# Products of attention pairs with their reciprocals, pinned behind first-layer units

## The chip, the cores and the metric

One Trainium2 chip, one core. The metric is device time in microseconds (us). A core has four engines that compute, each with its own instruction queue that runs in order: TensorE (PE, matrix multiplication), VectorE (DVE), ScalarE (ACT) and GpSimd (POOL). SyncE (SP) only issues transfers here, POOL issues them as well. An engine waits for another by a semaphore.

## What is computed

Three stages in a row: a linear attention, a layer that takes the maximum of three products, and a second feed-forward layer.

```python
def _attn_ref(q, k, v, w_phi):              # q, k, v: 4 batches, 8 heads, 576 tokens, 64
    def phi(x):
        proj = np.einsum('bhsd,df->bhsf', x, w_phi)
        proj = proj - np.max(np.abs(proj), axis=-1, keepdims=True)
        return np.concatenate([np.exp(proj), np.exp(-proj)], axis=-1)
    q_p, k_p = (phi(q), phi(k))
    kv = np.einsum('bhsf,bhsd->bhfd', k_p, v)
    z = np.sum(k_p, axis=2)
    num = np.einsum('bhsf,bhfd->bhsd', q_p, kv)
    den = np.einsum('bhsf,bhf->bhs', q_p, z)[..., None] + 1e-06
    return num / den

def _moe_ref(x, w1, w2, w3, w_out):         # x: 2304 x 512; d_ff 768
    h = np.maximum(np.maximum(x @ w1, x @ w2), x @ w3)
    return h @ w_out

def _moe2_ref(x, w_in, w_out, alpha):       # d_ff 2048
    h = x @ w_in
    return (np.maximum(h, 0.0) + alpha * np.minimum(h, 0.0)) @ w_out
```

Where the change works is the line num / den of the attention, whose result is the x of the first layer.

## The kernel before

Heads are taken in pairs: 4 batches of 4 pairs, 16 in all. An fp32 operand is split into a rounded high part and the rest (hi, lo), and a product is made of three matmuls: weights hi with x hi, weights hi with x lo, weights lo with x hi.

The loop at L458 runs over the pairs. Iteration i loads pair i+1, runs `queries` of pair i-1 interleaved with `keys` of pair i, converts some weights of the first layer, and then runs three units of the first layer (`layer1`), from i = 4 on and with a lag of two units, so that 34 units are done in it. A unit is one half (288 tokens) of one batch times one of six blocks of d_ff; 48 units in all, 12 for a batch. It has three groups, one for each of w1, w2 and w3, and a group is 12 matmuls of 128x288 into one tile p: three for each of the batch's four pairs, with the pair last made in the end. ACT copies the first group's p (s, L441), DVE takes the maximum with the second (s, L442) and the third (ho, L444), and POOL stores ho (L446, into h_d). Batches 1 to 3 are units 12 to 23, 24 to 35 and 36 to 47.

`queries` ends with the division. PE leaves numerators and denominators in nd (ACT copies them there, L362); POOL moves the denominators to dc with two small transfers (L393) and the second head's numerators (L394); DVE takes the reciprocal (L396); POOL writes it to memory (r_d, L398) and reads it back as rows spread over the partitions (xr, L405, two transfers for each half of the tokens); DVE multiplies (xr, L407), ACT rounds to x hi (L70) and DVE makes x lo (L76). Pairs of the first batch but the last do that on POOL. There are three xr buffers, three nd buffers.

After the loop the last pair's `queries` runs, and then the tail loop (L627) with units 34 to 47. Unit 36 is the first that needs the last pair's x. Beside each unit of the tail two steps of `convert` prepare the weights of the following layers: SP loads a tile of 512 KB (st, L498, three buffers, the next load issued when a buffer is freed), ACT converts (wt, L83), DVE has four rows for it (L85, L87, L89 and L91, the last two read st) and forms differences (L519), and POOL parks results in memory (q_d, L532). Then comes the first layer's second product (L679).

What sets the order: the kernel is scheduled ahead of time by a list scheduler that keeps a simulated clock and picks for each engine by priority and readiness; `high_priority` moves a block ahead of others. `keep_in_program_order` keeps an instruction on its engine where the program has it.

Of the kernel before, what the change touches and what calls it, by code (L numbers as in the profile page):

```python
# [14 lines left out]
ALU = mybir.AluOpType  # L15
# [5 lines left out]
B, H, S, D = 4, 8, 576, 64  # L21
NPAIR = H // 2
# [7 lines left out]
CH = S // 2  # L30
# [23 lines left out]
def tile_kernel(ctx: ExitStack, tc: tile.TileContext, qT, kT, tails, v, w_phi, w1, w2, w3, w_out, w_in, w_out2, alpha, out):  # L54
# [11 lines left out]
    nc = tc.nc  # L66
# [8 lines left out]
    def sub(eng, dst, src, hi):  # L75
        eng.tensor_tensor(dst, src, hi.bitcast(F32), op=ALU.subtract)  # L76
# [37 lines left out]
    def bank(tag, bufs, nm):  # L114
        return ps.tile([P, 512], F32, tag=tag, bufs=bufs, name=nm)
# [4 lines left out]
    ap_ctx, lp_ctx = ExitStack(), ExitStack()  # L120
# [3 lines left out]
    def at(shape, dtype, name, tag=None, bufs=1):  # L124
        pool = ap if (tag or name) in KEYS_ONLY else lp
        return pool.tile(shape, dtype, name=name, tag=tag or name, bufs=bufs)
# [34 lines left out]
    def i_of(pair):  # L161
        return pair[0] * NPAIR + pair[1]

    def plain_kv(pair):
        return pair[0] < 2
# [102 lines left out]
    def products(dst, ops, **kw):  # L268
        for i, (x, y) in enumerate(ops):
            nc.tensor.matmul(dst, x, y, start=i == 0, stop=i == len(ops) - 1, **kw)  # L270
# [69 lines left out]
    def queries(pair):  # L340

        parts = ("q",) if plain_kv(pair) else ("qh", "ql")
        qf = []
        for n, (o, w) in enumerate(CHUNKS):
            qf.append([])
            for x in parts:
                tag = f"qh{n}" if x != "ql" and pair[1] % 2 * len(x) != 1 else f"ql{n}"
                qf[n].append(at([P, 2, 2, w], F32 if plain_kv(pair) else F32R, tag=tag, bufs=1, name=x))
        nd = [at([P, S], F32, tag="nd", bufs=3, name="nd") for _ in range(2)]

        def num(n):
            o, w = CHUNKS[n]
            kv = kvs_of[pair]
            for h in range(2):
                pn = bank("p1", 3, "pn") if pair[0] == 0 else bank("pn", 1, "pn")
                ops = []
                for s in range(2):
                    q_ = [t[:, h, s] for t in qf[n]]
                    k_ = [t[:, h, s] for t in kv]
                    ops += [(k_[0], x) for x in q_] + [(x, q_[0]) for x in k_[1:]]  # L360
                products(pn[:, :w], ops)
                A.activation(nd[h][:, o : o + w], pn[:, :w], AF.Copy)  # L362

        def tail():
            yield 2, (0,), tail_of[pair]

        for g, tiles, pp in chain(project_queries(pair), tail()):
            o, w = (0, 2 * P, SM)[g], ST if g == 2 else 2 * P
            pt = bank("pn" if pair[0] == 0 and g == 1 else "pt", 1, "pt")
            for i in range(len(tiles)):  # L370
                for h in range(2):
                    c = h * len(tiles) * P + i * P
                    nc.tensor.transpose(pt[:, c : c + P], pp[:, 2 * i + h], ident)  # L373
            n = min(g, 1)
            dst = [t[:, :, :, o - CHUNKS[n][0] : o - CHUNKS[n][0] + w] for t in qf[n]]
            if plain_kv(pair):
                e = dst[0]
            else:
                e = at([P, 2, 2, 256], F32, tag="qe", bufs=2, name="qe")[:, :, :, :w]
            pv = pt[:, : 256 * len(tiles)].rearrange("p (h s) -> p h s", h=2)[:, :, -w:]  # L380
            A.activation(e[:, :, 0], pv, AF.Exp)
            A.activation(e[:, :, 1], pv, AF.Exp, scale=-1.0)
            if not plain_kv(pair):
                (hi_dve if g == 1 else hi_act)(dst[0], e)
                sub(V, dst[1], e, dst[0])
            yield
            if g != 1:
                num(n)
        yield
        dc = at([P, S // D], F32, tag="dc", bufs=2, name="dc")  # L390
        for h in range(2):
            dr = D * (1 - h)
            nc.gpsimd.dma_start(dc[h * D : (h + 1) * D], nd[h][dr : dr + 1].rearrange("a (p n) -> a p n", p=D))  # L393
        nc.gpsimd.dma_start(nd[0][D:], nd[1][D:])  # L394
        V.tensor_scalar(dc, dc, EPS, None, op0=ALU.add)
        V.reciprocal(dc, dc)  # L396
        rows = r_d[pair[0], pair[1]]
        nc.gpsimd.dma_start(rows.rearrange("h (p n) -> (h p) n", p=D), dc)  # L398
        res = []
        for c in range(2):  # L400
            cs = slice(c * CH, (c + 1) * CH)
            xr = raw_tile()
            for h in range(2):
                r = slice(h * D, (h + 1) * D)
                nc.gpsimd.dma_start(xr[r], rows[h : h + 1, cs].to_broadcast([D, CH]))  # L405
            e = G if i_of(pair) < NPAIR - 1 else V
            e.tensor_tensor(xr, nd[0][:, cs], xr, op=ALU.mult)  # L407
            xh, xl = x_tiles(c)
            if e is G:
                G.tensor_copy(xh, xr)  # L410
            else:
                hi_act(xh, xr)
            sub(e, xl, xr, xh)
            res.append((xh, xl))
        xs[pair[0]].append(res)

    def raw_tile():
        return xs_.tile([P, CH], F32, tag="xr", bufs=3, name="xr")
# [8 lines left out]
    def layer1(b, c, f, x, w, spread=False):  # L427
        pw = []
        for j in range(3):
            if spread:  # L430
                p = bank(("pn", "pt", "kv")[j], 1, "p1")
            else:
                p = bank("p1", 3, "p1")
            ops = []
            for k in range(KT):
                ks = slice(k * P, (k + 1) * P)
                ops += three(w[j][:, 0, ks], w[j][:, 1, ks], *x[k][c])
            products(p[:, :CH], ops)
            pw.append(p)
        s1 = xs_.tile([P, CH], F32, tag="s1", bufs=2, name="s1")  # L440
        A.activation(s1, pw[0][:, :CH], AF.Copy)  # L441
        V.tensor_tensor(s1, pw[1][:, :CH], s1, op=ALU.max)  # L442
        ho = xs_.tile([P, CH], F32, tag="ho", bufs=2, name="ho")
        V.tensor_tensor(ho, pw[2][:, :CH], s1, op=ALU.max)  # L444
        o = b * S + c * CH
        nc.gpsimd.dma_start(h_d[f, :, o : o + CH], ho)  # L446

    pairs = [(b, pr) for b in range(B) for pr in range(NPAIR)]
# [9 lines left out]
    for i, pair in enumerate(pairs):  # L458
        if i + 1 < len(pairs):
            load_pair(pairs[i + 1])  # L460
        with tc.high_priority(offset=(0, SOON, NOW, NOW)[pair[0]]):
            if i == PLAIN - 1:
                hi_dve(wph, wraw)
                sub(V, wpl, wraw, wph)
            run(*([at_priority(LATER, queries(last))] if last else []), keys(pair))
            last = pair
        count = CONVERT_IN[i] if i < len(CONVERT_IN) else 0
        for j in range(count):
            for _ in range(min(count, 4) if j == 0 else int(j + 3 < count)):
                fetch(begun[pair])  # L470
            with tc.high_priority(offset=LAST if i < NPAIR - 1 else 0):
                n = sum(len(x) for x in w)
                run(split_w123(n // 3, n % 3))
        u0 = 3 * (i - NPAIR) - LAG
        for u in range(u0, u0 + 3):
            if u >= 0:
                c, f = (u % 2, u // 2) if u < 12 else (u // NF1 % 2, u % NF1)
                layer1(u // 12, c, f, xs[u // 12], w[f])
    ap_ctx.close()
    sp = ctx.enter_context(tc.tile_pool(reuse_waits="tile", name="sp", bufs=1, side="right"))  # L480
    with tc.high_priority(offset=NOW):
        run(queries(last))
    lp_ctx.close()
    ring2 = ctx.enter_context(tc.tile_pool(reuse_waits="tile", name="ring2", bufs=10, side="right"))
    hp_ctx = ExitStack()
    hp = hp_ctx.enter_context(tc.tile_pool(reuse_waits="tile", name="hp", bufs=1, side="right"))

    def granule(pool, nm):

# [137 lines left out]
    for u in range(3 * (len(pairs) - NPAIR) - LAG, 12 * B):  # L627
        c, f = u // NF1 % 2, u % NF1
        layer1(u // 12, c, f, xs[u // 12], w[f], u % 2 == 0)
        with tc.high_priority(offset=LATER):  # L630
            convert(2)
        if u == 12 * B - NF1 - 1:
            for kk in range(NF1 // 2):
                load_h(0, kk)
            for kk in range(NF1 // 2):
                early.append(fetch_h(1, kk))
# [30 lines left out]
    for c in range(2 * B):  # L667
# [7 lines left out]
        for ms in ((0, 1), (2, 3)) if c == 0 else (range(KT),):  # L675
            for k, m in ((k, m) for k in range(NF1) for m in ms):
                cs = slice(m * P, (m + 1) * P)
# [169 lines left out]
    for block in range(nblocks):  # L847
# [4 lines left out]
        for half in range(2):  # L852
# [5 lines left out]
            for i in ORDER:  # L858
                for f in range(4):
                    ts_ = slice(f * T, (f + 1) * T)  # L860
                    r = wq[2 * half + f // 2, i]
                    cs = slice(f % 2 * 256, f % 2 * 256 + 256)
# [83 lines left out]
```

## Time and profile before

| | us |
|---|---|
| median of three runs | 875.53 |
| the runs | 874.87, 875.53, 876.23 |
| the profiled execution | 875.7 |
| its span | 873.9 |

Busy time over the span is 867.7 us for PE (99%), 683.1 for DVE (78%), 490.4 for ACT (56%) and 158.6 for POOL (18%). The costliest line is the matmul L270 with the tile p, 1728 matmuls of the first layer, 250.4 us of PE. The profile's names leave out buffer numbers, so p or xr stands for all tiles of that name. A line of a helper (L270, L70, L76, L83 to L91) stands for all its callers; the tile's name tells them apart.

### The profile page before, as it was taken

How to read it: one execution, taken by the hardware profiler on the slowest of the kernel's cores; microseconds unless marked ns; L12 is line 12 of the kernel's file. 1: busy time of each engine (PE TensorE's matmuls, PEld its weight loads, DVE VectorE, ACT ScalarE, POOL GpSimd, SP SyncE). 2: the span in 40 equal slices, each digit the busy share in tenths (PEclk: the TensorE clock that was granted, in tenths of full speed). 3: DMA queues.
4: the chain of work that ended last, by engine and by line, in shares of the span. 5: the costliest groups of instructions: out<-in, count | busy, mean ns of one | idle time of the engine just before them, and what ended most of it. 6: DMA issues, size and time to landing. Idle time of an engine off the chain costs nothing.

```text
span 873.9 us, 17484 instructions
## 1 busy us (share of the span) xinstructions
PE 867.7 (99%) x6631; PEld 854.8 (98%) x6631; DVE 683.1 (78%) x1290; ACT 490.4 (56%) x1017; POOL 158.6 (18%) x278
## 2 busy tenths in 40 slices
PE   9999999999999999999999999999999999999998
PEld 8898999999999999999999999999999999999998
DVE  4579888976888878888999755746478999987781
ACT  4666757677777762334455354646477763544440
POOL 0355222202222235521100101111111000000000
PEclk9999999999999999999999999999999999999999
DMA  6445544223323137996578853746248746533321
GB/s 235 134 165 161 170 125 154 64 63 95 92 74 103 37 115 258 323 320 199 178 247 270 258 174 133 241 168 203 109 138 275 261 153 189 171 123 122 121 74 49
DMA packets 70437, 143.00 MB, mean 164 GB/s; under 512 B 9152, under 2 KB 36176, under 8 KB 70352
## 3 DMA queue, kind: packets, MB, share of 16 engines
q1 hardware_dynamic: 53664, 92.95, 34.3%
q0 software_dynamic: 14816, 45.26, 15.1%
q10 hardware_dynamic: 1872, 3.67, 1.2%
q8 instruction: 52, 0.85, 0.4%
q14 instruction: 33, 0.27, 0.1%
HBM read 93.07 MB, written 46.34 MB: 160 GB/s over the span
## 4 chain that ended last, share of the span: by engine, by line
PE 94%; DVE 3%; DMA 1%; ACT 0%; issue 0%; POOL 0%; DVEq 0%; POOLq 0%; ACTq 0%
PE p L270 26%; PE acc L865 21%; PE sums L777 12%; PE p L679 9%; PE pc L777 6%; PE pj L270 5%; PE pn L270 5%; PE kvp L311 3%; PE pb L777 3%; PE kvp L298 3%; PE pt L373 2%; DVE mx L217 1%; DMA dc<-nd 1%; PE kvt L330 0%; PE warm L135 0%
## 5 line engine op out<-in xcount | busy, mean ns | idle before, releaser
L270 PE MATMUL p<-x,w123t 128*128 128x288 f32 x1728 | 250.4, 298 | 0.0
L270 PEld LDWEIGHTS p<-x,w123t 128*128 128x128 f32 x1728 | 234.8, 188 | 1.4 <-DVE ho L444 0.3
L777 PE MATMUL sums<-x,wi 128*128 128x288 f32 x768 | 107.6, 295 | 0.0
L865 PE MATMUL acc<-wq,o 128*128 128x256 f32 x864 | 105.5, 283 | 0.0
L865 PEld LDWEIGHTS acc<-wq,o 128*128 128x128 f32 x864 | 104.2, 189 | 0.0
L777 PEld LDWEIGHTS sums<-x,wi 128*128 128x128 f32 x768 | 103.9, 188 | 0.0
L865 PE MATMUL acc<-wq,x 128*128 128x256 f32 x648 | 78.1, 280 | 0.0
L865 PEld LDWEIGHTS acc<-wq,x 128*128 128x128 f32 x648 | 77.0, 188 | 0.0
L679 PE MATMUL p<-x,wo 128*128 128x288 f32 x576 | 76.6, 295 | 0.0
L679 PEld LDWEIGHTS p<-x,wo 128*128 128x128 f32 x576 | 76.5, 188 | 0.0
L796 DVE SCALAR_TENSOR_TENSOR g<-neg,al,g 128x576 f32<-128x576 f32 x64 | 50.3, 812 | 23.6 <-ACT neg L795 23.6
L217 DVE TENSOR_REDUCE mx<-pj 128x4 f32<-128x512 f32 (+1 forms) x80 | 49.8, 629 | 15.6 <-PE pj L270 15.3
L785 ACT ACTIVATE s<-sums 128x576 f32<-128x576 f32 x48 | 31.1, 647 | 42.0 <-PE sums L777 41.9
L797 POOL DMA_DIRECT2D g_d<-g x32 | 22.9, 715 | 166.8 <-DVE g L796 144.7
L446 POOL DMA_DIRECT2D h_d<-ho x48 | 27.1, 564 | 123.5 <-DVE ho L444 103.5
L83 ACT ACTIVATE wt<-st 128x512 f32<-128x512 f32 x38 | 25.2, 674 | 36.0 <-DMA st<-in_w_out 18.9
L250 ACT ACTIVATE ke<-pj,mx 128x128 f32<-128x128 f32 x96 | 36.6, 382 | 13.8 <-DVE mx L217 13.6
L795 ACT ACTIVATE neg<-g 128x576 f32<-128x576 f32 x64 | 40.2, 676 | 6.2 <-DVE g L827 5.9
L298 PEld LDWEIGHTS kvp<-v,ke 128*128 128x128 f32 x320 | 40.3, 191 | 2.4 <-ACT ke L251 0.5
L298 PE MATMUL kvp<-v,ke 128*128 128x128 f32 x320 | 42.3, 277 | 0.1
L441 ACT ACTIVATE s<-p 128x288 f32<-128x288 f32 x48 | 19.7, 413 | 40.3 <-PE p L270 36.4
L70 ACT ACTIVATE o<-wt 128x512 fp32r<-128x512 f32 x45 | 27.4, 627 | 25.0 <-PE acc L865 15.9
(161 smaller groups left out, 1819.6 us busy)
## 6 DMA issues: line engine op xcount, KB each, us to landing
g_d<-g POOLq DMA_DIRECT2D x32, 576.0 KB, 4.0
a<-g_d SPq DMA_DIRECT2D x36, 512.0 KB, 4.6
st<-in_w_out SPq DMA_DIRECT2D x22, 512.0 KB, 5.2
wst<-in_w SPq DMA_DIRECT2D x18, 512.0 KB, 4.2
st<-in_w_in SPq DMA_DIRECT2D x16, 512.0 KB, 4.3
yr<-y_d SPq DMA_DIRECT2D x28, 288.0 KB, 3.6
v<-in_v SPq DMA_DIRECT2D x16, 480.0 KB, 4.7
q_d<-wt POOLq DMA_DIRECT2D x28, 256.0 KB, 5.9
```

Of the source, the lines that this page charges most:

```text
L70: A.activation(dst, src, AF.Copy)
L217: V.tensor_reduce(mx, pv, axis=AX.X, op=ALU.max, apply_absolute_value=True, negate=True)
L250: A.activation(ev[:, a, 0], pv[:, a], AF.Exp, bias=mx[:, a : a + 1])
L270: nc.tensor.matmul(dst, x, y, start=i == 0, stop=i == len(ops) - 1, **kw)
L298: nc.tensor.matmul(kvp[:, j * P : (j + 1) * P], e[:, c], rv[:, t, j // 2 : j // 2 + 2].rearrange("p a d -> p (a d)"), start=first, stop=t ...
L446: nc.gpsimd.dma_start(h_d[f, :, o : o + CH], ho)
L679: nc.tensor.matmul(p2[m // 2][1][:, m % 2], x, y, start=k + n == 0, stop=k == NF1 - 1 and n == 2)
L777: nc.tensor.matmul(dst[:, j], a, b, start=start and n == 0, stop=n == len(ops) - 1, skip_group_check=True)
L785: A.activation(s, src, AF.Copy)
L795: A.activation(neg, gv[:, j], AF.Relu, scale=-1.0)
L796: V.scalar_tensor_tensor(gv[:, j], neg, al[:, f + j : f + j + 1], gv[:, j], op0=ALU.mult, op1=ALU.add)
L865: nc.tensor.matmul(acc[i], x, y, start=half == 0 and f == 0 and n == 0 and place[i][1] == 0, stop=half == 1 and f == 3 and n == 2, skip_gr ...
```

## The change

The product, the rounding and the difference are taken out of `queries` into a function `make_x`, and `queries` leaves its pair in a list `waiting`. For the first batch's pairs and the last pair of the second and third batch `make_x(False)` is called at once, as before. The other nine pairs of the loop wait until three units of `layer1` have been written, and their products are pinned there with `keep_in_program_order`. The last pair waits for unit 34, the first unit of the tail, and the pools ring2 and hp are opened behind it.

```diff
-        res = []
+        raw = []
         for c in range(2):
             xr = raw_tile()
             for h in range(2):
                 ...
+            raw.append(xr)
+        waiting.append((pair, nd[0], raw))
+        if pair[0] == 0 or pair[1] == NPAIR - 1 and pair != pairs[-1]:
+            make_x(False)
+    waiting = []
+    def make_x(pinned=True):
+        pair, num_, raw = waiting.pop(0)
+        res = []
+        for c, xr in enumerate(raw):
             e = G if i_of(pair) < NPAIR - 1 else V
-            e.tensor_tensor(xr, nd[0][:, cs], xr, op=ALU.mult)
+            x = e.tensor_tensor(xr, num_[:, c * CH : (c + 1) * CH], xr, op=ALU.mult)
+            if pinned:
+                tc.keep_in_program_order(x)
...
                 layer1(u // 12, c, f, xs[u // 12], w[f])
+        if waiting:
+            make_x()
     ap_ctx.close()
...
     with tc.high_priority(offset=NOW):
         run(queries(last))
-    lp_ctx.close()
-    ring2 = ctx.enter_context(tc.tile_pool(reuse_waits="tile", name="ring2", bufs=10, side="right"))
-    hp_ctx = ExitStack()
-    hp = hp_ctx.enter_context(tc.tile_pool(reuse_waits="tile", name="hp", bufs=1, side="right"))
...
     for u in range(3 * (len(pairs) - NPAIR) - LAG, 12 * B):
         c, f = u // NF1 % 2, u % NF1
         layer1(u // 12, c, f, xs[u // 12], w[f], u % 2 == 0)
+        if waiting:
+            make_x()
+            lp_ctx.close()
+            ring2 = ctx.enter_context(tc.tile_pool(reuse_waits="tile", name="ring2", bufs=10, side="right"))
+            hp_ctx = ExitStack()
+            hp = hp_ctx.enter_context(tc.tile_pool(reuse_waits="tile", name="hp", bufs=1, side="right"))
         with tc.high_priority(offset=LATER):
             convert(2)
```

In the changed kernel the product is L419, s is L455 and L456, ho L458, its store L460, the staging load L510, the differences L531 and their parking L544. The orders of all engines are the same up to a group of the first batch at about 108 us, and again from the first matmul of the second product (L679 before) on.

PE, at the joint of the third and the fourth batch. p_5081 is the last group of unit 35; p_5126, p_5139 and p_5152 are unit 36, p_5191, p_5204 and p_5217 unit 37. Before:

```order
L270 MATMUL p_5081<-x,w123t 128x288 x12
L270 MATMUL p_5126<-x,w123t 128x288 x12
L270 MATMUL p_5139<-x,w123t 128x288 x12
L270 MATMUL p_5191<-x,w123t 128x288 x6
L270 MATMUL p_5152<-x,w123t 128x288 x12
L270 MATMUL p_5191<-x,w123t 128x288 x6
L270 MATMUL p_5204<-x,w123t 128x288 x12
```

And now:

```order
L270 MATMUL p_5081<-x,w123t 128x288 x12
L270 MATMUL p_5126<-x,w123t 128x288 x9
L270 MATMUL p_5139<-x,w123t 128x288 x9
L270 MATMUL p_5152<-x,w123t 128x288 x9
L270 MATMUL p_5191<-x,w123t 128x288 x9
L270 MATMUL p_5204<-x,w123t 128x288 x9
L270 MATMUL p_5217<-x,w123t 128x288 x9
L270 MATMUL p_5126<-x,w123t 128x288
L270 MATMUL p_5139<-x,w123t 128x288
```

The six groups of units 36 and 37 are cut behind their ninth matmul, and the rest of them, one and then two matmuls each, follows in turn.

DVE, around the last pair's first product (xr_4963; x_4967 is its x). ho_4767 belongs to unit 31, the s1 behind the product to unit 32. Before:

```order
L444 TENSOR_TENSOR ho_4767<-p1_4751,s1_4764 128x288
L91 SCALAR_TENSOR_TENSOR wt_5372<-st_5256,wt_5372 128x512
L519 TENSOR_TENSOR wt_5381<-wt_5372,wt_5323 128x512
L519 TENSOR_TENSOR wt_5307<-wt_5372,wt_5307 128x512
L85 TENSOR_SCALAR wt_5386<-wt_5386 128x512
L407 TENSOR_TENSOR xr_4963<-nd_4868,xr_4963 128x288
L442 TENSOR_TENSOR s1_4809<-p1_4783,s1_4809 128x288
L87 TENSOR_SCALAR wt_5386<-wt_5386 128x512
L76 TENSOR_TENSOR x_4967<-xr_4963,x_4967 128x288
```

And now. The rows ahead of these, from the back: the two L89, two L87 and two L85 of wt_5443 and wt_5451, and ho of unit 35. Staging tiles take three buffers in turn, in the order st_5321, st_5378, st_5392, st_5449.

```order
L91 SCALAR_TENSOR_TENSOR wt_5443<-st_5321,wt_5443 128x512
L91 SCALAR_TENSOR_TENSOR wt_5451<-st_5378,wt_5451 128x512
L531 TENSOR_TENSOR wt_5459<-wt_5443,wt_5451 128x512
L85 TENSOR_SCALAR wt_5508<-wt_5508 128x512
L87 TENSOR_SCALAR wt_5508<-wt_5508 128x512
L89 SCALAR_TENSOR_TENSOR wt_5508<-st_5392,wt_5508 128x512
L91 SCALAR_TENSOR_TENSOR wt_5508<-st_5392,wt_5508 128x512
L531 TENSOR_TENSOR wt_5517<-wt_5508,wt_5459 128x512
L531 TENSOR_TENSOR wt_5443<-wt_5508,wt_5443 128x512
L85 TENSOR_SCALAR wt_5522<-wt_5522 128x512
L87 TENSOR_SCALAR wt_5522<-wt_5522 128x512
L419 TENSOR_TENSOR xr_4963<-nd_4868,xr_4963 128x288
```

The product has moved from between units 31 and 32 to behind unit 35 and the conversions up to half of wt_5522's.

POOL, from the write of the last pair's reciprocals (r_d) on. ho_4449 is a store of unit 29; ho_5017 is one of unit 34, ho_5097 one of unit 35. Before:

```order
L398 DMA r_d_67<-dc_4956 128x9
L532 DMA q_d_70<-wt_5245 128x512
L532 DMA q_d_70<-wt_5171 128x512
L446 DMA h_d_66<-ho_4449 128x288
L532 DMA q_d_70<-wt_5250 128x512
L532 DMA q_d_70<-wt_5259 128x512
L405 DMA xr_4963<-r_d_67 64x288 x2
L405 DMA xr_4970<-r_d_67 64x288 x2
```

And now:

```order
L398 DMA r_d_67<-dc_4956 128x9
L460 DMA h_d_66<-ho_5017 128x288
L544 DMA q_d_70<-wt_5386 128x512
L544 DMA q_d_70<-wt_5395 128x512
L460 DMA h_d_66<-ho_5097 128x288
L405 DMA xr_4963<-r_d_67 64x288 x2
L405 DMA xr_4966<-r_d_67 64x288 x2
```

The reads of the rows have moved behind the store of unit 35.

## Rows read from the trace of the kernel before

**Rows 1.** The page, 40 slices: granted TensorE clock, tenths of full speed.
```profile
PEclk9999999999999999999999999999999999999999
```

**Rows 2.** Busy us (x instructions) of each engine by stage, clock, DMA share, GB/s.
```profile
60.00:100.00 40.00, 38.44 (x266) 34.82 (x265) 36.15 (x83) 30.04 (x87) 16.40 (x27) 1.00 0.51 157
100.00:338.00 238.00, 238.00 (x1847) 235.67 (x1846) 196.69 (x403) 162.25 (x402) 62.87 (x114) 1.00 0.34 100
338.00:378.00 40.00, 40.00 (x303) 40.00 (x303) 35.71 (x76) 11.15 (x22) 18.23 (x35) 1.00 0.93 316
378.00:436.00 58.00, 57.97 (x438) 57.73 (x438) 53.17 (x112) 25.48 (x50) 10.67 (x19) 1.00 0.68 218
```

**Rows 3.** Chain of work 360 to 440: start us, us, what.
```profile
382.38 53.48 PE p L270 x402
```

**Rows 4.** Timeline, ACT, 374 to 384: start us, us, instruction, [idle before <- releaser].
```profile
375.24 0.41 ACT L441 ACTIVATE s<-p 128x288 f32<-128x288 f32 x1 [2.10 <-PE p L270]
```

**Rows 5.** Timeline, DVE, 364 to 370.
```profile
366.08 0.42 DVE L85 TENSOR_SCALAR wt<-wt 128x512 f32<-128x512 f32 x1
366.41 0.45 DVE L407 TENSOR_TENSOR xr<-nd,xr 128x288 f32<-128x288 f32 x1
```

**Rows 6.** Timeline, ACT, 360 to 368.
```profile
364.85 0.68 ACT L83 ACTIVATE wt<-st 128x512 f32<-128x512 f32 x1 [0.47 <-DMA st<-in_w_out]
366.90 0.45 ACT L70 ACTIVATE x<-xr 128x288 fp32r<-128x288 f32 x1 [1.37 <-DVE xr L407]
```

**Rows 7.** Waits of DVE, whole span: us in total, times, longest us.
```profile
DVE xr L407 <- DMA xr<-r_d: 7.8, 7, 1.8
```

**Rows 8.** Line L405, 300 to 375: issue of the reciprocals' rows to landing.
```profile
DMA to landing us min/median/max: 2.6/3.7/5.1
```

**Rows 9.** Timeline, DVE, 335 to 346.5.
```profile
335.89 0.42 DVE L85 TENSOR_SCALAR wt<-wt 128x512 f32<-128x512 f32 x1
336.34 0.43 DVE L87 TENSOR_SCALAR wt<-wt 128x512 uint32<-128x512 uint32 x1
...
341.49 0.76 DVE L85 TENSOR_SCALAR wt<-wt 128x512 f32<-128x512 f32 x2
342.16 0.45 DVE L444 TENSOR_TENSOR ho<-p,s 128x288 f32<-128x288 f32 x1
342.53 0.75 DVE L87 TENSOR_SCALAR wt<-wt 128x512 uint32<-128x512 uint32 x2
343.19 1.29 DVE L89 SCALAR_TENSOR_TENSOR wt<-st,wt 128x512 uint32<-128x512 uint32 x2
344.40 1.29 DVE L91 SCALAR_TENSOR_TENSOR wt<-st,wt 128x512 uint32<-128x512 uint32 x2
```

**Rows 10.** Line L498, 335 to 385: issue of a staging load to landing.
```profile
DMA to landing us min/median/max: 4.8/6.1/8.8
```

**Rows 11.** Line L498, 300 to 436: the same.
```profile
DMA to landing us min/median/max: 3.3/4.8/8.8
```

**Rows 12.** Timeline, POOL, 340 to 400.
```profile
357.15 2.07 POOL L405 DMA_DIRECT2D xr<-r_d  x4 [0.71 <-DMA r_d<-dc]
359.62 0.57 POOL L446 DMA_DIRECT2D h_d<-ho  x1 [0.40 <-DVE ho L444]
```

**Rows 13.** Timeline, PE, 0 to 14.
```profile
1.05 2.82 PE L135 MATMUL warm<-idle 128*128 128x64 f32 x12 [1.05 <-DVE signs L137]
3.79 3.63 PE L270 MATMUL pj<-wraw,k 128*128 128x256 f32 x8
...
11.37 1.03 PE L270 MATMUL pj<-wraw,k 128*128 128x256 f32 x4
```

**Rows 14.** Busy us by stage, the start: columns as in rows 2.
```profile
4.00:7.40 3.40, 3.40 (x8) 2.31 (x8) 1.93 (x5) 0.00 (x0) 0.19 (x1) 1.00 0.92 264
```

**Rows 15.** Timeline, PE, 60 to 96.
```profile
66.72 1.19 PE L270 MATMUL p<-x,w123t 128*128 128x288 f32 x6
...
84.38 0.39 PE L270 MATMUL pj<-wph,xhk 128*128 128x256 f32 x1 [0.83 <-DVE ppt L221]
```

More of the change, by code (lines that the diff above doesn't have):

```diff
@@ L398, in queries @@
         nc.gpsimd.dma_start(rows.rearrange("h (p n) -> (h p) n", p=D), dc)
-        res = []
+        raw = []
         for c in range(2):
-            cs = slice(c * CH, (c + 1) * CH)
             xr = raw_tile()
@@ L404, in queries @@
                 r = slice(h * D, (h + 1) * D)
-                nc.gpsimd.dma_start(xr[r], rows[h : h + 1, cs].to_broadcast([D, CH]))
+                src = rows[h : h + 1, c * CH : (c + 1) * CH]
+                nc.gpsimd.dma_start(xr[r], src.to_broadcast([D, CH]))
+            raw.append(xr)
[7 more added lines that the diff above has]
+        for c, xr in enumerate(raw):
             e = G if i_of(pair) < NPAIR - 1 else V
-            e.tensor_tensor(xr, nd[0][:, cs], xr, op=ALU.mult)
+            x = e.tensor_tensor(xr, num_[:, c * CH : (c + 1) * CH], xr, op=ALU.mult)
+            if pinned:
+                tc.keep_in_program_order(x)
             xh, xl = x_tiles(c)
```

## Prediction, with its working

> **What bounds the kernel now.** I read the rows in this order: the granted clock, the busy time by stage, the chain around the place where the order changes, then the engines that hand TensorE its data there. The clock is full in all 40 slices [rows 1]. By stages [rows 2], PE is busy 238.00 of 238 us from 100 to 338, all 40 from 338 to 378 and 57.97 of 58 from 378 to 436. A busy engine may still be slow, so I hold the pitch against it: around the joint of loop and tail the chain is matmuls alone, 402 in 53.48 us [rows 3], 0.133 us each. So in the stretch that the change touches (its orders on PE differ only between about 108 us and the first w_out matmul at about 436 us) TensorE is the bound at full speed with nothing to give back. What DVE, ACT or a queue saves there cannot shorten the span; what one of them makes PE wait for lengthens it, one for one, because all later stages follow on PE.
>
> The reader should see the other side as well: how early x is ready. The s copy of unit 35 starts at 375.24, released by that unit's first group [rows 4]; two groups of 12 remain, 24 x 0.133 = 3.2 us, so unit 36, the first that uses the last pair's x, starts at about 378.4. In the kernel before, that pair's first product starts at 366.41 [rows 5] and ACT rounds it to x hi at 366.90, done at 367.35 [rows 6]: 11 us early.
>
> **The change part by part.**
> No work is added or removed: the same products, the same DMAs, the same roundings. Of the nine pairs pinned in the loop, the product now stands on DVE behind the third unit of its iteration. What that removes is DVE standing in front of a product while the reciprocals' rows are on their way: 7.8 us in 7 waits over the whole kernel, none over 1.8 [rows 7]. PE waits for none of them [rows 2], so they are worth 0. What it adds is that these x are ready later. I went through the new orders between 108 and 360 us: wherever a group is split for a missing x, or an nd buffer is freed later by a later product, PE has at least 2 us of other matmuls in front of the need. I take 0. From below the bound is also 0 (PE is full there); from above I take one landing of the rows, 5.1 at the longest [rows 8].
>
> The last pair is another matter. Its product is pinned behind unit 34, and the new order of DVE puts it behind ho of unit 35 and the conversions of that unit and the next. PE's order says what this costs: after unit 35's last group, units 36 and 37 are issued as six pieces of 9, which is what needs three of the four pairs, and only then the matmuls with the last pair's x. That is 54 x 0.133 = 7.2 us of work that doesn't need it. The next matmul needs x hi.
>
> How late is x hi? Clock zero is the end of unit 35's last group.
> - The handover to DVE is 0.04, as from the product (end 366.86) to ACT (366.90) [rows 5, 6]. ho has the product's shape, 0.45 [rows 5]. Together 0.5.
> - Then seven conversion rows up to the L91 that frees the staging buffer: two L85 (from 341.49 to 342.16 with the next row, 0.67), two L87 (342.53 to 343.19, 0.66), two L89 (343.19 to 344.40, 1.21), one L91 (half of the pair's 1.29, 0.65) [rows 9]. 3.2, so 3.7.
> - SP can issue the load of the next staging tile only now: there are three buffers, and st_5449 is the third tile after st_5321, so takes its place. The new order needs this very tile before the product: L85 and L87 of wt_5522 stand ahead of it on DVE, and they need ACT's L83 of that tile. Landing took 4.8, 6.1 and 8.8 us (least, median, most) in 335 to 385 [rows 10], and 3.3, 4.8 and 8.8 in 300 to 436 [rows 11]. I take 6.1, since the load falls into the first of these stretches, where the DMA engines were busy 0.93 of the time [rows 2]. 9.8.
> - L83 takes 0.68 [rows 6]: 10.5. L85 to L87 of one tile is 0.45 (335.89 to 336.34) [rows 9], L87 to the next row 0.33, as 366.08 to 366.41 between an L85 and a product [rows 5]: 11.3. The product, 0.45: 11.7. Handover, x hi in 0.45 [rows 6], handover: 12.3.
>
> So PE stands still for 12.3 - 7.2 = 5.1 us. With the other landings it is 2.3 (3.3 us), 3.8 (4.8) and 7.8 (8.8). While it waits, the conversion rows between (five more, some 3 us) run inside the landing and cost nothing; if the landing were short they would be the cover that is gone, but 3.3 still hides them. What is late next: x lo, one DVE row behind x hi, has six matmuls (0.8 us) in front of it; nothing.
>
> The Trainium skill has a rule for a transfer's time (DMA: Bandwidth & Descriptors, "Anatomy of one DMA — SWDGE (gpsimd) path"): some 2.0 us fixed plus the bytes at 436 GB/s. It is for the GpSimd queue and one DMA by itself; for this 512 KB tile it gives an estimate of 3.2 us, a stall of 2.2, and 877.7. The rows differ from it, 6.1 at the median with the DMA engines nearly full, and I go by the rows.
>
> The other ingredient of the product is the rows of reciprocals. On POOL their issue moves from 357.15 [rows 12] to behind the store of unit 35's ho, so at 0.5 + 0.57 for that store [rows 12], and two issues (half of 2.07) later the first half's DMAs are out: 2.1. Landing takes 2.6 to 5.1, median 3.7 [rows 8]: 5.8. The product, x hi and two handovers add 0.98: 6.8, under 7.2. So POOL's path alone does not stall PE, and with 5.1 it does by 1.0; it is hidden behind the staging load either way. The later stages have room: the conversions for the first w_out matmul are the same in number, and the order from there on is that of before.
>
> Sum: 0 + 0 + 5.1. The profiled run took 875.7 with a span of 873.9 (1.8 around it), so it would come to 880.8 with a span of 879.0; the median of the three runs is 0.2 lower, so I forecast 875.53 + 5.1 = 880.6.
>
> **The rivals.**
> *A, PE falls back to the pace of its start.* After an idle time of 1.05 us PE starts slowly: from 3.79 on eight pj matmuls of 256 columns take 3.63 us (0.454 each), and at 11.37 four take 1.03 (0.258) [rows 13]. The granted clock reads 1.00 in that stretch too [rows 14], full speed or 2.4 GHz, so here the pace tells it and not that column; 0.454 to 0.258 is near the step to 1.2 GHz. In the middle of the kernel I found no idle time longer than 0.83 [rows 15], so no row shows what 5 us does. If PE is slow after the gap for as long as at the start (1.05 to about 7.4, 6.4 us), half of that is lost, 3.2 us: 883.8. For it speaks that the gap would be by far the longest; against it, that no row behind the start shows a fall.
> The Trainium skill (TensorE: Matmul & The Clock Gate, "What's actually happening") says that the throttled state is the default, that activity releases it and idleness brings it back. By that rule A would hold, at 883.8; the start of this trace agrees with its first half only.
>
> *B, no stall.* The staging tile may be there in time after all, if DVE frees its buffer sooner than I think or DVE runs ahead of PE. Then POOL's path decides, 6.8 against 7.2, and the time is 875.5. For it: the least landing, 3.3, leaves 2.3 us, so the whole rest of the chain would have to be 2.3 shorter. Against it: each link stands in the in-order queue of one engine. That the pins do nothing at all (product issued where it was) gives the same 875.5.
>
> *C, more waits.* The nine pins in the loop cost PE too, where I found 2 us of cover; one rows' landing above that cover, 5.1 - 2 = 3.1, in one place gives 883.7.
>
> *D, faster.* Mechanism: DVE freed of its waits before products serves PE sooner between 60 and 100 us, the only stage near the change where PE idles: 38.44 of 40 [rows 2], the longest wait, 0.83, for DVE's ppt [rows 15], and the six matmuls at 66.72 take 1.19 instead of 0.80. All idle time gone is 1.6, with as much again hidden in slow pitches 3.1: 873.9 to 872.4. It decides only if the last pair's x costs under 1.6. Against it: the order of every engine is the same up to about 108 us, and batch 0's products aren't pinned.
>
> **How the numbers follow.** The stall of 2.3 to 7.8 us with the pace held has 0.53 (877.8 to 883.3, 880.6 the middle of it by the median landing); A 0.21 (with the same landings 881.0 to 886.5); C 0.09; B 0.13; D 0.04. The range 877.0 to 886.0 takes in the forecast, C and all but the end of A, and leaves out B, D and that end, under 0.2. A measurement of this kernel tells about 0.2%, 1.75 us, from no change. Faster: D, 0.04. Same: B, 0.13. Slower: the rest, 0.83.
>
> **What would show it.** Right: one idle stretch on PE of about 5 us, 7.2 us behind unit 35's last group (about 385 us into the span), released by ACT's x hi; ahead of it on DVE the product without a wait for xr, behind L85 and L87 that waited for ACT's L83, which waited for an st load; DVE's 7.8 us in front of products mostly gone; before 378 us PE full. A shows as 288-column matmuls at some 0.26 instead of 0.133 just behind, or a granted clock below 1. C shows as PE idle between 110 and 378. Wrong would be: the gap's releaser is POOL's rows or nothing, or the staging tile landed long before DVE came to it.

## Result: 10 us slower, and the profile after

The changed kernel takes 885.43 us (median of four runs, 884.20 to 885.85) against 875.47 for the kernel before; the ratio is 1.0111, with a 95% interval of 1.0093 to 1.0129. Its profiled execution took 885.04, with a span of 883.3; before it was 873.9 [rows 2 to 4 are of that span], so 9.4 us are to be found.

The page of the changed kernel, PE's busy tenths and the granted clock in 40 slices of 22.1 us:

```profile
PE   9999999999999999979999999999999999999998
...
PEclk9999999999999999989999999999999999999999
```

One slice stands out in both, that from 375 to 397: PE at 7 tenths, the clock at 8. By stages (columns as in rows 2):

```profile
100.00:338.00 238.00, 236.64 (x1833) 233.82 (x1832) 189.24 (x385) 156.57 (x389) 55.69 (x102) 1.00 0.31 93
...
385.00:392.00 7.00, 2.22 (x17) 1.99 (x15) 4.84 (x10) 0.97 (x2) 2.85 (x5) 0.89 0.97 331
392.00:400.00 8.00, 7.13 (x38) 7.13 (x39) 7.91 (x19) 4.09 (x9) 1.89 (x3) 0.67 0.96 325
400.00:446.00 46.00, 46.00 (x350) 46.00 (x349) 43.10 (x91) 20.30 (x40) 6.19 (x10) 1.00 0.60 199
```

From 385 to 392 PE works 2.22 of 7 us. From 392 to 400 it is busy again, but the granted clock is 0.67 and 38 matmuls fit where 60 would. From 400 on all is as before. A smaller loss stands far ahead: 236.64 busy of 238 between 100 and 338, where before it was 238.00 [rows 2]. PE's waits (us in total, times, longest) name all three:

```profile
PE p L270 <- ACT x L70: 5.7, 1, 5.7
...
PE p L270 <- ACT w123t L70: 1.0, 1, 1.0
...
PE pn L270 <- ACT nd L362: 0.3, 1, 0.3
```

PE's timeline around the large one (start, us, instruction, idle time before it and who ended it):

```profile
369.73 17.49 PE L270 MATMUL p<-x,w123t 128*128 128x288 f32 x131
392.87 19.38 PE L270 MATMUL p<-x,w123t 128*128 128x288 f32 x129 [5.65 <-ACT x L70]
```

The count closes. Idle time before x hi: 5.65. The chain of waits counts 339 matmuls of L270 in 47.14 us behind the gap; at the 0.133 of [rows 3] they take 45.1, so the slow pace costs 2.05. The two short waits are 1.03 (at 174.42) and 0.34 (at 120.00). Together 9.07 of 9.4; 0.2 more stand in 60 to 100, 38.22 busy in place of 38.44 [rows 2].

Now the chain into x hi. DVE first, from ho of unit 35 on; the order of these rows is that printed ahead of the prediction:

```profile
380.54 0.45 DVE L458 TENSOR_TENSOR ho<-p,s 128x288 f32<-128x288 f32 x1
...
383.48 1.28 DVE L91 SCALAR_TENSOR_TENSOR wt<-st,wt 128x512 uint32<-128x512 uint32 x2
...
387.81 1.29 DVE L531 TENSOR_TENSOR wt<-wt 128x512 f32<-128x512 f32 x2
391.09 0.43 DVE L85 TENSOR_SCALAR wt<-wt 128x512 f32<-128x512 f32 x1 [1.98 <-ACT wt L83]
391.55 0.43 DVE L87 TENSOR_SCALAR wt<-wt 128x512 uint32<-128x512 uint32 x1
391.89 0.45 DVE L419 TENSOR_TENSOR xr<-nd,xr 128x288 f32<-128x288 f32 x1
```

ACT and SP at the same time (ACT: the conversion of that tile, then the rounding to x hi):

```profile
390.39 0.66 ACT L83 ACTIVATE wt<-st 128x512 f32<-128x512 f32 x1 [5.08 <-DMA st<-in_w_out]
392.38 0.78 ACT L70 ACTIVATE x<-xr 128x288 fp32r<-128x288 f32 x2 [1.32 <-DVE xr L419]
```

```profile
384.23 3.94 SPq L510 DMA_DIRECT2D st<-in_w_out  x3
```

Read it from the end. x hi at 392.38 follows the product at 391.89. The product follows L87 by 0.34 and that follows L85 by 0.46, DVE's own pitch. L85 waited 1.98 for ACT's L83 at 390.39, and that waited 5.08 for a staging tile. SP had issued this load at 384.23, right behind the first of the two L91 rows (half of 1.28 from 383.48: 384.12): 6.1 us to landing, the median taken in the prediction [rows 10].

The chain of waits tells it otherwise, and here it misleads. Its last pieces before x hi:

```profile
385.06 6.79 DMA q_d<-wt
391.84 0.05 issue
391.89 0.46 DVE xr L419
```

It puts the product down to a parking transfer (q_d) that landed in the same tenth of a microsecond. The product starts 0.34 behind the row ahead of it, as such rows do when nothing is waited for, and has no idle time in DVE's timeline; the only wait is two rows earlier. The reciprocals' rows, what the product does need from POOL, were issued from 382.53 on and landed 3.5 to 5.6 us later. The first half's two issues are the second row below; they landed 4.4 and 4.0 us after their starts, by 387.1, well ahead of the product:

```profile
377.24 0.54 POOL L398 DMA_DIRECT2D r_d<-dc  x1 [1.13 <-DVE wt L87]
...
382.53 1.05 POOL L405 DMA_DIRECT2D xr<-r_d  x2 [0.40 <-DMA r_d<-dc]
```

```profile
DMA to landing us min/median/max: 3.5/4.2/5.6
```

The first of these two rows is worth more than the second. It is the write of the last pair's reciprocals, and before it stood here:

```profile
350.00 0.54 POOL L398 DMA_DIRECT2D r_d<-dc  x1
```

Now it is at 377.24, 27 us later. Something far ahead of the tail made the pair late.

### The profile page after: what moved, and what is told of

The parts are those of the page before. It is cut to its first block, busy times and chain, and to the rows that moved or that the text cites. A ratio compares the mean times of both kernels' runs of the same rounds, so it can differ in the third digit from the quotient of the medians.

```text
span 883.3 us, 17499 instructions
## 1 busy us (share of the span) xinstructions
PE 869.9 (98%) x6631; PEld 857.0 (97%) x6631; DVE 683.4 (77%) x1290; ACT 488.2 (55%) x1017; POOL 159.8 (18%) x278
## 4 chain that ended last, share of the span: by engine, by line
PE 90%; DMA 4%; DVE 3%; issue 1%; POOL 1%; ACT 1%; SPq 0%; POOLq 0%; ACTq 0%; DVEq 0%
PE p L270 23%; PE acc L883 20%; PE sums L795 12%; PE p L697 9%; PE pc L795 6%; PE pj L270 5%; PE pn L270 5%; PE kvp L311 3%; PE pb L795 3%; PE kvp L298 2%; PE pt L373 2%; DMA dc<-nd 1%; DMA q_d<-wt 1%; DMA r_d<-dc 1%; DMA v<-in_v 1%
## 5 line engine op out<-in xcount | busy, mean ns | idle before, releaser
L270 PE MATMUL p<-x,w123t 128*128 128x288 f32 x1728 | 253.2, 300 | 6.7 <-ACT x L70 5.7
L270 PEld LDWEIGHTS p<-x,w123t 128*128 128x128 f32 x1728 | 236.9, 190 | 8.3 <-ACT x L70 5.9
L460 POOL DMA_DIRECT2D h_d<-ho x48 | 27.8, 580 | 120.3 <-DVE ho L458 107.6
L83 ACT ACTIVATE wt<-st 128x512 f32<-128x512 f32 x38 | 24.9, 671 | 30.6 <-DMA st<-in_w_out 17.0
L362 ACT ACTIVATE nd<-pn 128x256 f32<-128x256 f32 (+1 forms) x64 | 26.8, 424 | 27.1 <-PE pn L270 23.4
L405 POOL DMA_DIRECT2D xr<-r_d x64 | 33.9, 535 | 39.9 <-DMA r_d<-dc 24.7
```

Source lines behind the costliest of these rows:

```text
L405: nc.gpsimd.dma_start(xr[r], src.to_broadcast([D, CH]))
```

## What the experiments tell apart

Two theories. **P** is the prediction's: the pin of the last pair behind unit 34 puts its product behind the conversions. **N** came from those 27 us: the pins in the loop do it. A product that stands behind a unit's ho on DVE holds its numerator's buffer (nd, three of them) until then; the copies of the next pairs' numerators wait for a buffer, and the whole attention chain of the last batch slides back. Times are medians of 4 to 10 runs, ratios are to runs of the kernel before on the same chip.

**The last pair's pin taken out.**

```diff
-        if pair[0] == 0 or pair[1] == NPAIR - 1 and pair != pairs[-1]:
+        if pair[0] == 0 or pair[1] == NPAIR - 1:
             make_x(False)
```

The pools ring2 and hp are opened right behind the last pair's queries again, as in the kernel before.

> The changed kernel, but the last pair's products are formed at the end of its queries as before, without a pin; the nine pins in the loop stay. Theory P (the prediction: the pin behind unit 34 makes the last pair's x late) expects the idle time of 5.65 us on PE and the slow matmuls behind it to vanish: 885.4 less 5.65 and some 2, about 877.5. Theory N (the nine pins make it late, through the nd buffers: the copies of a pair's numerators wait until an earlier pinned product has freed a buffer, so the last pair's reciprocals come 27 us later) expects no change: 885.4, with the same idle time at about 387.

886.42 us, ratio 1.0124 (1.0109 to 1.0139): as slow as with the pin. PE's wait for x hi is 6.85 us here, and on DVE the twelve rows ahead of the product are the same: the scheduler puts the product there without being told to. P falls.

**Only the last pair pinned, the nine as before.**

```diff
-        if pair[0] == 0 or pair[1] == NPAIR - 1 and pair != pairs[-1]:
+        if pair != pairs[-1]:
             make_x(False)
```

> Only the last pair's product is pinned, behind unit 34; the nine pairs of the loop are as before. Theory P expects the idle time on PE before unit 36's tenth matmul, 5 us or more, and 880.6 to 885.4. Theory N expects the reciprocals of the last pair at about 350 as before, no idle time there and 875.5.

875.03, ratio 0.9998 (0.9989 to 1.0008). The pin does move the product, from 366.41 [rows 5] to here:

```profile
380.16 0.45 DVE L419 TENSOR_TENSOR xr<-nd,xr 128x288 f32<-128x288 f32 x1
```

ACT's x hi is done at 381.08. Five of the six groups of units 36 and 37 are cut behind their ninth matmul here too, 45 x 0.133 = 6.0 us of work behind about 378.4, so it is needed at about 384.4 and is there 3 us ahead. PE is full where the gap was (columns as in rows 2):

```profile
378.00:392.00 14.00, 14.00 (x107) 14.00 (x107) 12.68 (x28) 5.92 (x12) 4.49 (x8) 1.00 1.00 352
```

So neither the pin nor the cut groups, which the prediction took for the sign of the stall, cost anything by themselves.

**One pin alone, that of pair 1 of the last batch.**

```diff
-        if pair[0] == 0 or pair[1] == NPAIR - 1 and pair != pairs[-1]:
+        if pair not in ((3,1),):
             make_x(False)
```

with the last pair's products at once and the pools opened as before.

> One pin alone: pair 1 of the last batch (the third counting from the end), pinned behind the third unit of its iteration; everything else as before. Theory N expects that this pin by itself holds an nd buffer long enough: the copies of a numerator in 300 to 360 pause for 10 us or more, the last pair's x is late, PE idles some 5 to 8 us at about 387, 881 to 886. A rival of N (the delays of all nine pins add up, none suffices by itself) and theory P expect 875.5 and no idle time there.

879.69, ratio 1.0058 (1.0042 to 1.0075): slower, as N has it, but less than the 881 to 886 expected. The mechanism of N, in ACT's timeline of this kernel (the copies of numerators; between them there is none):

```profile
327.19 0.38 ACT L362 ACTIVATE nd<-pn 128x256 f32<-128x256 f32 x1 [1.52 <-PE pn L270]
...
357.72 0.39 ACT L362 ACTIVATE nd<-pn 128x256 f32<-128x256 f32 x1 [0.87 <-DVE xr L419]
```

30.5 us without a copy, ended by DVE's pinned product (line L419 is that product). Before, copies came every 4 us in this stretch, and these were the last two:

```profile
334.56 0.44 ACT L362 ACTIVATE nd<-pn 128x320 f32<-128x320 f32 x1 [3.00 <-PE pn L270]
338.61 0.44 ACT L362 ACTIVATE nd<-pn 128x320 f32<-128x320 f32 x1 [1.25 <-PE pn L270]
```

In the changed kernel a pause stands at 324.30 to 340.62, on ACT (the last row is the last pair's last copy) and on DVE:

```profile
324.30 0.38 ACT L362 ACTIVATE nd<-pn 128x256 f32<-128x256 f32 x1
...
340.05 0.67 ACT L83 ACTIVATE wt<-st 128x512 f32<-128x512 f32 x1
340.62 0.37 ACT L362 ACTIVATE nd<-pn 128x256 f32<-128x256 f32 x1
...
367.30 0.44 ACT L362 ACTIVATE nd<-pn 128x320 f32<-128x320 f32 x1 [2.18 <-PE pn L270]
```

```profile
338.16 0.46 DVE L458 TENSOR_TENSOR ho<-p,s 128x288 f32<-128x288 f32 x1
338.53 0.45 DVE L419 TENSOR_TENSOR xr<-nd,xr 128x288 f32<-128x288 f32 x1
...
339.87 0.45 DVE L419 TENSOR_TENSOR xr<-nd,xr 128x288 f32<-128x288 f32 x1
```

The first product is behind ho (338.16), the second ends at 340.32, and the copy starts when ACT is free of its conversion, at 340.62. PE is not idle meanwhile, it takes units of the first layer instead; that is why a look at PE's cover alone showed nothing. What comes out later is the last pair. One pin gives less than nine: PE's gap is 2.39, not 5 to 8, and its matmuls behind it are slow too, 54 in 8.94 us:

```profile
387.22 8.94 PE L270 MATMUL p<-x,w123t 128*128 128x288 f32 x54 [2.39 <-ACT x L70]
```

```profile
388.00:390.00 2.00, 2.00 (x10) 2.00 (x9) 1.68 (x5) 0.53 (x1) 0.00 (x0) 0.50 1.03 398
```

**A fourth nd buffer, all pins kept.**

```diff
-        nd = [at([P, S], F32, tag="nd", bufs=3, name="nd") for _ in range(2)]
+        nd = [at([P, S], F32, tag="nd", bufs=4, name="nd") for _ in range(2)]
```

> The changed kernel with all its pins and a fourth nd buffer. Theory N expects the pause in the copies of numerators near 330 to vanish, the last pair's reciprocals some 15 us or more earlier, no idle time at 387 and no slow matmuls: 875.5 to 877 (the two short waits near 120 and 174 may stay, 1.4 us). Theory P expects the idle time to stay, since the pin behind unit 34 stays: 880 to 885.4.

878.01, ratio 1.0032 (1.0020 to 1.0044). The gap at 387 is gone with the pin of the last pair still in place, and the clock is full:

```profile
378.00:392.00 14.00, 14.00 (x108) 14.00 (x107) 12.76 (x29) 4.94 (x11) 4.75 (x9) 1.00 0.87 295
```

The pair's reciprocals are written at 363.40, 14 us earlier than at 377.24. So the buffer carries the delay, 14 us of the 27 by this comparison (a better one follows with the last kernel of four buffers). The three xr buffers may carry some of the rest (the second half's rows of a pair are issued 10 us behind the first's, at 340.41 and 330.17, in the changed kernel); that was not tried apart. The time is above the expected 875.5 to 877; in the profiled execution, the shortest of the six at 877.06, PE waits 0.95 near 173.

**Is that wait the pins'?** Two kernels were meant to tell: the fourth buffer without pins in the second batch, and pins in the second batch alone with three buffers.

```diff
-        if pair[0] == 0 or pair[1] == NPAIR - 1 and pair != pairs[-1]:
+        if pair[0] <= 1 or pair[1] == NPAIR - 1 and pair != pairs[-1]:
```

> The fourth nd buffer again, and the three pairs of the second batch unpinned; the pins of the third and fourth batch and of the last pair stay. If the two short waits of PE near 120 and 174 come from the pins in the second batch, they vanish and with them the rest of the loss: 875.0 to 875.8. If they come from the rest, 876.5 to 878.

877.22 (runs from 875.84 to 879.36), ratio 1.0021 (1.0011 to 1.0031), not 875.0 to 875.8. The wait is there. In the profiled execution, the longest of the ten, it is even longer, and the 21 matmuls behind it take 4.58 us where they took 3.05:

```profile
174.74 4.58 PE L270 MATMUL p<-x,w123t 128*128 128x288 f32 x21 [1.91 <-ACT w123t L70]
```

So I ran the kernel before with the fourth buffer and nothing else.

> The kernel before, without a pin, with a fourth nd buffer: a control for the two kernels with four of them. If the fourth buffer by itself lets the attention run ahead of the weights' conversions and so makes the wait near 174, that wait of 1 to 2 us is here too and the time is 876.5 to 877.5. If the wait comes from pins alone, it is absent and the time is 875.2.

876.96 (runs from 875.98 to 880.80), ratio 1.0022 (1.0010 to 1.0033), with the same wait and not one pin:

```profile
174.04 3.04 PE L270 MATMUL p<-x,w123t 128*128 128x288 f32 x21 [1.22 <-ACT w123t L70]
```

The fourth buffer costs some 1.5 us by itself, half of e4's 2.85; the other half lies within what the two intervals leave open. So e4's time is no measure of the pins. How the buffer costs it is not shown: attention does not run ahead, as I had expected, since the last numerator's copy is at 349.67 here and was at 338.61, and the rounding of the weight that PE waits for starts at 173.38 where it was at 169.25.

For the delay this kernel is the better comparison. With four buffers the last pair's reciprocals are written at 359.09 without a pin and at 363.40 with all of them (e4): the pins cost 4.3 us there, and 27 with three buffers.

```diff
-        if pair[0] == 0 or pair[1] == NPAIR - 1 and pair != pairs[-1]:
+        if pair not in ((1,0), (1,1), (1,2),):
             make_x(False)
```

(three buffers, the last pair at once, the pools opened as before)

> Only the three pairs of the second batch are pinned, three nd buffers. If their pins cost the two short waits (0.34 near 120, 1.03 near 174) and nothing else, 876.5 to 877.0, with no idle time at 387. If the late x of the last pair begins with them, an idle time of some us at 387 and over 879.

879.08, ratio 1.0040 (1.0025 to 1.0055). Both short waits are there, 0.42 at 119.57 and 0.95 at 173.90, and no gap at 387. But the time is 2 us above the range. Waits that I had not expected make up as much: 1.55 between 338 and 378 and 0.38 at 388.83; 1 us more of the profiled execution was not traced. PE in the first of these stretches, and the row of DVE just ahead of the first (others stand between the rows shown):

```profile
349.74 13.98 PE L270 MATMUL p<-x,w123t 128*128 128x288 f32 x103 [0.30 <-DVE s L456]
364.51 2.54 PE L270 MATMUL p<-x,w123t 128*128 128x288 f32 x17 [0.79 <-ACT s L455]
```

```profile
347.93 0.46 DVE L419 TENSOR_TENSOR xr<-nd,xr 128x288 f32<-128x288 f32 x1 [1.46 <-DMA xr<-r_d]
```

A product waits 1.46 us for its rows on DVE, and the maximum that frees PE's tile stands behind it. So the costs of single pins do not simply add up to that of all.

**Pins in the third and fourth batch, three buffers.**

```diff
-        if pair[0] == 0 or pair[1] == NPAIR - 1 and pair != pairs[-1]:
+        if pair[0] <= 1 or pair[1] == NPAIR - 1:
```

> Six pins: the pairs of the third and fourth batch, with three nd buffers; the second batch and the last pair are as before. If the two short waits near 120 and 174 belong to the pins of the second batch (with three buffers), PE is full from 100 to 338. The late x of the last pair stays with its idle time of 5 us or more at 387 and the slow matmuls behind it: 882 to 885. If the second batch's pins have a part in the idle time, it is shorter than 5 us.

886.41, ratio 1.0125 (1.0109 to 1.0141). No short waits, PE full from 100 to 338, and the largest gap of all, 8.83 us:

```profile
100.00:338.00 238.00, 238.00 (x1846) 235.69 (x1845) 190.26 (x389) 157.88 (x392) 56.90 (x104) 1.00 0.32 94
```

```profile
393.54 4.69 PE L270 MATMUL p<-x,w123t 128*128 128x288 f32 x18 [8.83 <-ACT x L70]
```

With three buffers the short waits come with the second batch's pins, the gap with the later batches'. The time is above the expected range since the gap is longer, not shorter, without the second batch's pins: on DVE the product stands behind three more conversion rows (390.50 to 392.56). The profiled execution is the longest of the four, 888.19.

**Which link ends last at 387?** Four staging buffers in the changed kernel.

```diff
-        return sp.tile(shape, dtype, tag="st", bufs=3, name=nm)
+        return sp.tile(shape, dtype, tag="st", bufs=4, name=nm)
...
-        return sp.tile([P, 512], F32, tag="wt", bufs=8, name="wt")
+        return sp.tile([P, 512], F32, tag="wt", bufs=6, name="wt")
```

> The changed kernel with four staging buffers (and six conversion tiles in place of eight, for the room). The staging load in front of the last pair's product is then issued one conversion earlier, at about 380 in place of 384. If the load is the link that ends last, DVE's wait of 1.98 us in front of that conversion vanishes and PE's idle time falls from 5.65 to some 3.7: what is left are DVE's own rows, which the product stands behind. 883.0 to 883.6 with the slow stretch kept. If the reciprocals' rows (POOL's path) are the link, the idle time stays at 5.65 and the time at 885.4.

883.93 (881.79 to 884.96), ratio 1.0095 (1.0079 to 1.0110), 0.3 above the expected range. In the profiled execution, the shortest of the four, DVE no longer waits in front of L85, and PE's gap is 3.57, as expected of the staging load:

```profile
386.59 1.29 DVE L531 TENSOR_TENSOR wt<-wt 128x512 f32<-128x512 f32 x2
387.80 0.42 DVE L85 TENSOR_SCALAR wt<-wt 128x512 f32<-128x512 f32 x1
388.25 0.43 DVE L87 TENSOR_SCALAR wt<-wt 128x512 uint32<-128x512 uint32 x1
388.60 0.45 DVE L419 TENSOR_TENSOR xr<-nd,xr 128x288 f32<-128x288 f32 x1
```

```profile
389.58 18.00 PE L270 MATMUL p<-x,w123t 128*128 128x288 f32 x122 [3.57 <-ACT x L70]
```

The load ended last, by 2 us; behind it stand DVE's own conversions. The spread of the runs is wide, and the gap of the longer ones isn't known, so the time alone says less than the rows.

**Why are the matmuls slow behind the gap?** The gap filled with matmuls.

```diff
-    def layer1(b, c, f, x, w, spread=False):
+    def layer1(b, c, f, x, w, spread=False, fill=0):
...
+            for n in range(fill if j == 0 else 0):
+                nc.tensor.matmul(p[:, :CH], w[0][:, 0, :P], x[0][c][0], start=n == 0, stop=n == fill - 1)
             products(p[:, :CH], ops)
...
-        layer1(u // 12, c, f, xs[u // 12], w[f], u % 2 == 0)
+        layer1(u // 12, c, f, xs[u // 12], w[f], u % 2 == 0, 44 if u == 36 else 0)
```

> The changed kernel with 44 extra matmuls of 128x288 (5.85 us) ahead of unit 36's first group; they write into its tile before the group starts anew, so nothing is computed from them. They cover the idle time of 5.65 us. If the idle time is what makes the matmuls behind it slow (rival A of the prediction), no stretch at half pace follows, and the time is 885.4 - 5.65 - 2.05 + 5.85 = 883.6. If the slow stretch has another cause at that place (the full DMA engines, for one), it stays and the time is 885.6.

884.58 (884.48 to 884.64), ratio 1.0105 (1.0090 to 1.0120). The clock stays at 1.00 with the DMA engines as full as before:

```profile
390.00:394.00 4.00, 3.88 (x30) 3.65 (x29) 2.68 (x6) 2.02 (x4) 0.05 (x1) 1.00 1.03 418
394.00:398.00 4.00, 3.52 (x26) 3.12 (x24) 3.60 (x10) 1.76 (x5) 1.09 (x2) 1.00 0.94 307
398.00:402.00 4.00, 3.73 (x28) 3.66 (x28) 3.71 (x9) 1.71 (x4) 1.30 (x2) 1.00 1.02 339
```

So the idle time is what takes the clock down, not the load on the DMA engines. The time, 1.0 above the 883.6 expected for this and 1.0 below the 885.6 of the rival, would not have told the two apart; the clock does. The extra are three new short waits (0.12, 0.48 and 0.27 of the 4 us in each row), 0.87 in all, the two longer ones for ACT's copy of a first group.

## Why the prediction came out as it did

The sign, the place on PE and the range were right; the likeliest time, 880.6, was 4.8 us too low, and the cause that it gave was wrong.

- **The bound.** PE is the bound, nothing could be gained, and each wait added lengthened the span one for one: 9.3 of 9.4 us are idle or slow time of PE. DVE's 7.8 us in front of products [rows 7] did go, all but 1.2, and PE got none of them. Part of it turned up again in front of the reciprocals, where DVE had waited 3.7 before:

```profile
DVE dc L395 <- DMA dc<-nd: 9.1, 7, 3.3
...
DVE xr L419 <- DMA xr<-r_d: 1.2, 1, 1.2
```

- **The stall at unit 36.** Forecast 5.1 (its links add up to 5.0), measured 5.65, by the chain that was laid out: ho, seven conversion rows, a staging load, L83, L85, L87, product, x hi. From the end of unit 35's last group (387.22 - 7.17 = 380.05) ho starts 0.49 later, not 0.04, since DVE still had a difference to do; L91 ends at 384.12 (4.1 for a forecast 3.7), the load takes 6.1 as forecast, and SP's issue and the rest add 0.2. That the load took just the median is luck: those of the stretch took 4.8 to 8.8 [rows 10], and in e1, by the same chain, the gap was 6.85.
- **What lies under the load.** The step "five more, some 3 us" of conversion rows is wrong. From the first L91 to the second difference it is eight rows, 384.12 to 389.1, 5.0 us. With the least landing, 3.3, the stall would have been some 3.7 and not 2.3; e6 shows it, 3.57. So the lower end of the sum, 877.8, was some 1.4 too low.
- **POOL's path.** Forecast at 5.8 from clock zero to the rows' landing, it took 7.0 (380.05 to 387.1). The term left out is the write of the reciprocals, 5.0 us in the chain of waits from 377.24: the first half's issue waited for it until 382.53 and not for the store of ho alone. With the 0.98 that follow this is 8.0, not 6.8: above the 7.2 of cover, so POOL's path alone would have stalled PE by 0.8. It was hidden behind the load, as the prediction had allowed for.
- **The cause.** The step that failed is "The last pair is another matter. Its product is pinned behind unit 34". e1 and e2 show that this pin costs nothing. The nine pins in the loop, of which the prediction says "I take 0", cost all of it. That the stall came out near the forecast size is luck in its cause: the chain in the tail was read rightly off the new order, but what put the product there was not. The error was in how I looked at the nd buffers: I asked whether PE has 2 us of other work where a buffer comes free late. It has, always, but the last pair's numerators then come 29 us later (the last copy is at 367.30 in place of 338.61), and that moves its reciprocals, rows and product into the tail, where conversions are queued in front. The new order showed the result, and I charged it to the pin nearest by.
- **Rival A**, given 0.21, came true: the mean granted clock is 0.67 from 392 to 400 and reads 0.50, the lower of its two levels, 1.2 GHz, from 393 to 397. It was sized at 3.2 us from the start of the kernel and measured 2.05. This and the next point are most of the miss of 4.8: 2.05 + 1.37 + 0.55 for the stall.
- **Rival C** came true in small: 1.37 in two places in the second batch, where I had taken 0. By e8 and e10 they come with the pins there; how is not shown, for e9 has waits of the same two kinds without a pin. The cover of 2 us that I had found was of the products; the waits are for a weight's rounding (ACT, w123t) and a numerator's copy that stood behind other work.
- **B and D** are out: the load ended last, and the stage from 60 to 100 lost 0.2 us and gained none.

The Trainium skill (DMA: Bandwidth & Descriptors, "Anatomy of one DMA — SWDGE (gpsimd) path") gave an estimate of 3.2 us for the load; the load that mattered took 6.1 on SP's queue with the DMA engines busy 0.97 of the time from 385 to 392. The Trainium skill (TensorE: Matmul & The Clock Gate, "What's actually happening") says that idleness brings the throttled state back; the trace agrees, 0.50 behind 5.65 us of idle time, and e5 shows it by taking the idle time away. Behind 0.95 to 1.22 us of it the clock read 1.00.

## What to carry over

A product that is pinned later holds its inputs' buffers longer; follow each buffer to who waits for it and on to the end of that chain, even where the bound engine has other work meanwhile. Where the new order of an engine shows something late, undo the parts of the change one by one before charging it to the part that stands next to it: the order that the scheduler gives to one part alone can be read before any run. And read a chain of waits against the engine's own timeline: a row that starts at its usual pitch behind the row ahead of it waited for nothing.

## What the runs showed of the hardware

PE's granted clock fell behind some idle times and not behind others. Behind 0.95 (e4), 1.03 (the changed kernel at 174) and 1.22 us (e9) it read 1.00, and the next 21 matmuls took 3.04 to 3.05 us, which is full pace (21 x 0.133 = 2.8 and the end of the last). Behind 1.91 us (e7) they took 4.58 and the clock fell to 0.50, behind 2.39 (e3) it read 0.50, and behind 3.57, 5.65, 6.85 and 8.83 (e6, the changed kernel, e1, e10) it read 0.50 as well for 2 us or more. In most of them the fall costs about as much: 1.5 us (e7, 4.58 less 3.05), 1.6 (e6, 21 matmuls in 4.64), 1.8 (e3, 54 matmuls in 8.94 less 7.17) and 2.05 (the changed kernel). So idle times of 1.91 and 2.39 us cost 3.4 and 4.2 in all. In e10 it costs about 4: the clock reads 0.50 until 402 and 1.00 only from 402.5, with a further idle time of 0.71 us in between, at 398.94.

At the start of the kernel the pace is near half as well (0.454 for 0.258), with a granted clock of 1.00 [rows 13, 14]; behind these gaps the column does show the fall. Why it differs at the start was not tried.
